# Six pieces of weights instead of three taken apart before the MLPs begin, 2.5 instead of 2 per step, batch 1's attention one step later

## The chip, the cores and the metric

The kernel runs on one core of a Trainium2 chip. The metric is the device time of one execution in microseconds (us). PE is the matmul engine, PEld its weight load, DVE the vector engine, ACT the scalar engine, SP the engine whose queue issues nearly all DMAs. In this chip's profile a granted PE clock of 1.00 stands for the higher of its two levels (2.4 GHz) and 0.50 for the lower (1.2 GHz).

## The reference

```python
# q, k, v: (4 batches, 8 heads, 576, 64); heads 0-3 a local mask (stride 32), heads 4-7 a strided mask
scores = scale * (q @ k.T), masked, softmax
attn_out = softmax @ v                          # (B, H, S, D)
x = attn_out.transpose(0, 2, 1, 3).reshape(2304, 512)
for w_in, w_out in two layers:                  # (512, 2048), (2048, 512)
    h = np.maximum(x @ w_in, 0.0)
    x = (h * h) @ w_out
```

All in float32; the weights and the result are compared at float32 accuracy, so each product is made of three matmuls on rounded high and low parts.

## The kernel before

**The weights' pieces.** The weights arrive as 64-bit words. A layer has 32 pieces of 128 x 512 words, in the order in which they are needed: the `in` piece for column group 0, the `out` piece for row group 0, `in` 1, `out` 1 and so on. Each is taken apart by four operations: `sign_and_end` (two DVE instructions, L213 and L216), `exponent_range` (ACT, L222), `together` (DVE, L227), `in_parts` (ACT L240 makes the high part, DVE L241 the low part). The list `conv` staggers them: in its steady part each run of four operations starts one piece, carries two on and finishes the one that was begun three earlier. `conv_by(n)` issues the next n operations of the list; one whose piece has not been loaded stops it. `ready(key)` issues what is missing if a matmul needs a piece that is not finished in program order.

**The start.** Batch 0's attention (12 fills of packed heads) runs alone, in 15 rounds of eight rows of the table ALONE. After each round the tables START_LOAD and START_CONV say how many pieces are loaded and how many operations of `conv` are issued: 19 in all, which finishes three pieces (0, 1, 2). Batch 0 uses DVE and ACT for its masks, maxima, exponents and divisions, and they are in-order engines, so the pieces' operations stand in the same queues.

**The MLPs.** 72 steps per layer. Step s issues the first product of step s+1 (`mm1`, 12 matmuls, from an `in` piece), then the second product of step s (`mm2`, 12 matmuls, from an `out` piece). Behind `mm1` ACT forms the ReLU and its square (r, sq, gh; L688, L693, L694) and DVE the low part gl (L698). A step has eight points (three inside `mm1`, one behind it, three inside `mm2`, one behind it). At each, `point()` issues the attention of the next batch as far as it is due, and, while the 32 pieces of layer 0 are not done, one operation of `conv`: eight per step, that is two pieces, just what a step uses. The attention of batch 1 is spread by `spans` over points 0 to 116 (steps 0 to 14), that of batches 2 and 3 over the next blocks.

**What sets the order.** Python's order is the order on each engine: there is no scheduler (`manual_schedule`). SP's queue is in order too: `load_ahead(4)` stands at the head of each step, the attention's own loads stand where a fill has freed a buffer.

Of the kernel before, what the change touches and what calls it, by code (L numbers as in the profile page):

```python
# [23 lines left out]
NF = DFF // P  # L24
# [6 lines left out]
NB = len(BLOCKS[0])  # L31
# [10 lines left out]

N_PT = 8

START_LOAD = (0, 0, 0, 1, 0, 1, 0, 1, 0, 1, 1, 1, 1, 2, 2)
START_CONV = (0, 0, 0, 0, 0, 0, 0, 0, 0, 2, 3, 3, 3, 4, 4)
GAP = 80

FIRST_2 = 2
# [93 lines left out]
def tile_attention_then_two_mlps(  # L143
# [34 lines left out]
    half1 = len(pieces) // 2  # L178
# [3 lines left out]
    def load_piece():  # L182

        n = n_load[0]
        if n >= len(pieces):
            return
        kind, layer, f = pieces[n]
        raw[n] = wpool.tile([P, 512, 2], I32, tag=f"w{n % half1}", name="raw")
        n_load[0] += 1
        dst = raw[n].rearrange("p n w -> p (n w)")  # L190
        if kind == "in":
            dst = dst.rearrange("p (c m) -> p c m", c=KC)
            src = w_in[layer].rearrange("(c p) m -> p c m", p=P)[:, :, 2 * f * P:2 * (f + 1) * P]
        else:
            src = w_out[layer][f * P:(f + 1) * P, :]
        nc.sync.dma_start(out=dst, in_=src)

    def load_ahead(n):

        while n and n_load[0] < min(half1, n_part[0] + AHEAD):  # L200
            load_piece()
            n -= 1
# [46 lines left out]
    n_conv, n_part = [0], [0]  # L249

    def conv_by(n):

        while n and n_conv[0] < len(conv):
            fn, i = conv[n_conv[0]]
            if i >= n_load[0]:
                return
            fn(i)
            n_conv[0] += 1
            n -= 1
            n_part[0] += fn is in_parts  # L260
# [25 lines left out]
    def load_qk():  # L286
        i = n_in[0]
        if i >= NFILL:
            return
        n_in[0] += 1  # L290
        qk = src_of(i)[0]
        tag = "qk" + str(i % 3 if i < SPLIT else 0)
        kin[i] = fpool.tile([P, QKW if tag == "qk2" else 4 * KW], F32, tag=tag, name="qk", bufs=1)
        nc.sync.dma_start(out=kin[i][:, :qk.shape[-1]], in_=qk)
# [76 lines left out]
    def load_v():  # L371
        i = n_vin[0]
        if i >= NFILL:
            return
        n_vin[0] += 1
        _, v = src_of(i)
        vin[i] = fpool.tile([P, VW], F32, tag="v", name="v", bufs=5)
        nc.sync.dma_start(out=vin[i][:, :v.shape[-1]], in_=v)
# [240 lines left out]
    def att_to(n):  # L619
        while n_att[0] < n:  # L620
            for fn, i in att[n_att[0]]:
                fn(i)
            n_att[0] += 1
# [31 lines left out]
    def block_x(k):  # L655
        layer, j = blocks[k]
        return (xh[j], xl[j]) if layer == 0 else xin[k]

    def mm1(s, point):

        if s >= len(steps):
            return
        k, f = steps[s]
        ne = tiles_of(k)
        n = TB // ne
        x_hi, x_lo = block_x(k)
        if n_att[0] < len(att):
            ps = ps_h.tile([P, TB], F32, tag="h", name="ps_h")
        else:
            ps = ps_a.tile([P, TB], F32, tag="a", name="ps_h")  # L670
        for c in range(KC):
            for e in range(ne):
                w = ready(("in", blocks[k][0], f + e))
                for i, (a, x) in enumerate(((0, x_hi), (0, x_lo), (1, x_hi))):

                    nc.tensor.matmul(  # L676
                        ps[:, e * n:(e + 1) * n],
                        lhsT=w[:, a, c * P:(c + 1) * P],
                        rhs=x[:, c, :n],
                        start=c == 0 and e == 0 and i == 0,  # L680
                        stop=c == KC - 1 and i == 2 and e == ne - 1,
                    )
                    one_small()
            if c < KC - 1:
                point()
        r = gpool.tile([P, TB], F32, tag="r", name="r", bufs=1)
        sq = gpool.tile([P, TB], F32, tag="sq", name="sq", bufs=1)
        nc.scalar.activation(out=r, in_=ps, func=AF.Relu, scale=W_BACK)  # L688
        h = gpool.tile([P, TB], F32R, tag="gh", name="gh", bufs=2)
        lo = gpool.tile([P, TB], F32R, tag="gl", name="gl", bufs=2)  # L690
        if 0 < n_load[0] - n_part[0]:

            nc.scalar.activation(out=sq, in_=r, func=AF.Square)  # L693
            nc.scalar.activation(out=h, in_=sq, func=AF.Copy)  # L694
        else:
            nc.scalar.activation(out=h, in_=r, func=AF.Square)  # L696
            nc.vector.tensor_tensor(out=sq, in0=r, in1=r, op=ALU.mult)  # L697
        nc.vector.tensor_tensor(out=lo, in0=sq, in1=r32(h), op=ALU.subtract)  # L698
        gh[s], gl[s] = h, lo

    def mm2(s, point):
        k, f = steps[s]
        layer, j = blocks[k]
# [51 lines left out]
                y_at.setdefault(s + 3 * i + 2 * c, []).append((fn, k, c))  # L755


    spans = [(b * NF * N_PT, ((b + 1) * NF - 1) * N_PT - 4) for b in range(3)]

    with tc.manual_schedule():  # L760
        nc.scalar.dma_start(out=cst, in_=consts)
        for n in range(5):
            if n < 3:
                load_qk()
            load_v()
        rounds = 0
        while n_att[0] < att_end[0]:
            att_to(min(n_att[0] + len(ALONE), att_end[0]))
            load_ahead(START_LOAD[rounds])
            conv_by(START_CONV[rounds])  # L770
            rounds += 1
        def nothing():
            pass

        mm1(0, nothing)
        for s in range(len(steps)):
            k, f = steps[s]
            layer, j = blocks[k]
            n_pt = [0]
            load_ahead(4)  # L780
            for fn, k2, c in y_at.get(s, ()):
                fn(k2, c)

            def point(s=s, layer=layer, j=j, f=f):
                n_pt[0] += 1
                at = N_PT * s + n_pt[0]
                for b, (p0, p1) in enumerate(spans):
                    if at > p0:
                        lo, hi = att_end[b], att_end[b + 1]
                        att_to(min(hi, lo + -(-(hi - lo) * (at - p0) // (p1 - p0))))  # L790
                if n_part[0] < half1 or (layer == 1 or j == NB - 1 and f > 2) and n_pt[0] % 4:
                    conv_by(1)

            mm1(s + 1, point)
            point()
            mm2(s, point)
            point()
            if layer == 0 and j == NB - 1:
                for _ in range(2):
                    load_piece()  # L800
# [36 lines left out]
```

## Time and profile before

| what | us |
|---|---|
| median of three runs | 936.99 (934.66 to 937.49) |
| the profiled execution | 935.01 |
| its span (first to last instruction) | 933.1 |
| PE busy | 899.3 (96%) |
| DVE busy | 459.8 (49%) |
| ACT busy | 410.8 (44%) |

The span is one launch on one core. Matmuls are pipelined and their ends are modelled, so the busy time of PE overlaps itself and the idle time in front of an instruction tells more than the share. The start of the program (0 to 40 us) is batch 0's attention; layer 0's steps follow, the first 15 of them (45 to about 175 us) with the taking apart of weights and batch 1's attention beside them.

### The profile page before, as it was taken

The numbers are of one execution on the slowest core, as the hardware profiler recorded it, in microseconds if no ns is written. First come the engines' busy times: TensorE is split into PE (matmuls) and PEld (weight loads), VectorE is DVE, ScalarE is ACT, GpSimd is POOL, SyncE is SP. The second block draws the span as 40 slices with busy tenths as digits, with TensorE's granted clock in tenths as the row PEclk, the third lists the DMA queues.
The fourth block names the chain that finished last, engine by engine and source line by source line (L and its number), as shares of the span: only waits on it lengthen the run. The fifth ranks groups of instructions, "written<-read, shape, count | busy, mean of one in ns | idle before, by whom it ended". The sixth has DMA issues, their size and how long they took to land.

```text
span 933.1 us, 12404 instructions
## 1 busy us (share of the span) xinstructions
PE 899.3 (96%) x4624; PEld 753.7 (81%) x4624; DVE 459.8 (49%) x1196; ACT 410.8 (44%) x863; POOL 0.2 (0%) x4
## 2 busy tenths in 40 slices
PE   8788888899999999999999999999999999999998
PEld 7666667687788888899888888888888888888897
DVE  5867677466675765422268877322222223222221
ACT  6666566355554554332367676332223222322222
POOL 0000000000000000000000000000000000000000
PEclk9799999999999999999999999999999999999999
DMA  8854351022222211010366530001001000100010
GB/s 255 292 168 147 129 182 42 29 84 74 68 91 77 88 46 56 1 47 1 125 213 208 199 113 12 12 27 41 15 9 69 1 22 1 57 6 6 1 46 23
DMA packets 43884, 71.91 MB, mean 77 GB/s; under 512 B 3504, under 2 KB 28208, under 8 KB 43824
## 3 DMA queue, kind: packets, MB, share of 16 engines
q1 hardware_dynamic: 43680, 70.86, 22.9%
q8 instruction: 37, 0.61, 0.3%
q10 hardware_dynamic: 144, 0.26, 0.1%
q14 instruction: 23, 0.19, 0.1%
HBM read 61.67 MB, written 9.44 MB: 76 GB/s over the span
## 4 chain that ended last, share of the span: by engine, by line
PE 88%; DVE 6%; ACT 4%; issue 1%; DMA 1%; SPq 0%; DVEq 0%; ACTq 0%
PE ps_h L676 43%; PE ps_y L731 37%; PE ps_o L477 3%; PE ps_s L418 2%; PE ps_pt L461 1%; ACT r L688 1%; PE ps_s L324 1%; DVE gl L698 1%; ACT sq L693 1%; DVE raw L216 1%; DVE w L241 1%; ACT gh L694 1%; PE ps_x L523 1%; DVE val L227 1%; DVE s L438 1%
## 5 line engine op out<-in xcount | busy, mean ns | idle before, releaser
L676 PE MATMUL ps_h<-xh,w 128*128 128x512 f32 (+1 forms) x1280 | 406.9, 378 | 18.3 <-DVE w L241 13.2
L676 PEld LDWEIGHTS ps_h<-xh,w 128*128 128x128 f32 x1280 | 234.8, 190 | 64.3 <-DVE w L241 18.4
L688 ACT ACTIVATE r<-ps_h 128x512 f32<-128x512 f32 x144 | 86.3, 599 | 406.0 <-PE ps_h L676 383.6
L676 PE MATMUL ps_h<-xl,w 128*128 128x512 f32 (+1 forms) x640 | 238.4, 373 | 0.0
L697 DVE TENSOR_TENSOR sq<-r 128x512 f32<-128x512 f32 x106 | 73.3, 692 | 328.5 <-ACT r L688 328.2
L731 PE MATMUL ps_y<-gh,w 128*128 128x512 f32 (+1 forms) x640 | 155.5, 375 | 0.0
L731 PE MATMUL ps_y<-w,gh 128*128 128x512 f32 x576 | 144.6, 389 | 0.0
L698 DVE TENSOR_TENSOR gl<-sq,gh 128x512 fp32r<-128x512 f32 x144 | 99.7, 692 | 79.3 <-ACT gh L694 65.3
L676 PEld LDWEIGHTS ps_h<-xl,w 128*128 128x128 f32 x640 | 121.9, 191 | 16.9
L731 PEld LDWEIGHTS ps_y<-w,gh 128*128 128x128 f32 x576 | 107.6, 188 | 22.0
L731 PEld LDWEIGHTS ps_y<-gh,w 128*128 128x128 f32 x640 | 108.4, 189 | 16.7
L731 PE MATMUL ps_y<-gl,w 128*128 128x512 f32 (+1 forms) x320 | 84.9, 374 | 0.0
L731 PE MATMUL ps_y<-w,gl 128*128 128x512 f32 x288 | 79.1, 389 | 0.0
L696 ACT ACTIVATE gh<-r 128x512 fp32r<-128x512 f32 x106 | 67.2, 634 | 3.4
L731 PEld LDWEIGHTS ps_y<-w,gl 128*128 128x128 f32 x288 | 54.0, 188 | 11.2
L731 PEld LDWEIGHTS ps_y<-gl,w 128*128 128x128 f32 x320 | 55.2, 189 | 8.9
L454 ACT ACTIVATE s<-s,m 96x128 f32<-96x128 f32 (+2 forms) x176 | 56.0, 387 | 5.1 <-DVE m L438 4.3
L477 PEld LDWEIGHTS ps_o<-v,pt 128*96 128x96 f32 (+2 forms) x352 | 44.7, 181 | 5.4 <-ACT pt L469 0.5
L241 DVE TENSOR_TENSOR w<-val,w 128x512 fp32r<-128x512 f32 x64 | 43.7, 684 | 4.1 <-ACT w L240 4.0
L222 ACT ACTIVATE raw<-raw 128x512 f32<-128x512 f32 x64 | 42.9, 670 | 6.1 <-DVE raw L216 6.1
L216 DVE SCALAR_TENSOR_TENSOR raw<-raw 128x512 int32<-128x512 int32 x64 | 44.4, 694 | 2.2
L477 PE MATMUL ps_o<-v,pt 128*96 128x65 f32 (+2 forms) x352 | 43.8, 258 | 0.1
(36 smaller groups left out, 582.0 us busy)
## 6 DMA issues: line engine op xcount, KB each, us to landing
raw<-moe_w_in_d SPq DMA_DIRECT2D x32, 512.0 KB, 5.1
raw<-moe_w_out_d SPq DMA_DIRECT2D x32, 512.0 KB, 3.8
qk<-loc_qk_d SPq DMA_DIRECT2D x12, 416.0 KB, 3.0
out_d<-o SPq DMA_DIRECT2D x18, 256.0 KB, 2.0
y_dram<-o SPq DMA_DIRECT2D x16, 256.0 KB, 2.0
y_in<-y_dram SPq DMA_DIRECT2D x16, 256.0 KB, 3.4
qk<-loc_qk_d SPq DMA_DIRECT2D x12, 304.0 KB, 3.6
v<-loc_v_d SPq DMA_DIRECT2D x24, 130.0 KB, 3.1
```

The source lines that it names most:

```text
L216: nc.vector.scalar_tensor_tensor(out=lower, in0=upper, scalar=-(2 ** 31), in1=lower, op0=ALU.bitwise_and, op1=ALU.bitwise_or)
L222: nc.scalar.activation(out=upper, in_=upper, func=AF.Copy, scale=2.0 ** (W_EXP // 8 - 112))
L241: nc.vector.tensor_tensor(out=w[:, 1], in0=v, in1=r32(w[:, 0]), op=ALU.subtract)
L418: nc.tensor.matmul(sv[:, h, g], lhsT=t[:, (h * ng + g) * nq:(h * ng + g + 1) * nq], rhs=t[:, 2 * ng * nq + g * ks:2 * ng * nq + g * ks + n ...
L454: nc.scalar.activation(out=blk, in_=blk, func=AF.Exp, scale=-1.0, bias=m[:nq, j:j + 1])
L477: nc.tensor.matmul(ps[:nq, j * W:(j + 1) * W], lhsT=pt[:nk, j * nq:(j + 1) * nq], rhs=t[:nk, j * W:(j + 1) * W], start=True, stop=True,)
L676: nc.tensor.matmul(ps[:, e * n:(e + 1) * n], lhsT=w[:, a, c * P:(c + 1) * P], rhs=x[:, c, :n], start=c == 0 and e == 0 and i == 0, stop=c ...
L688: nc.scalar.activation(out=r, in_=ps, func=AF.Relu, scale=W_BACK)
L696: nc.scalar.activation(out=h, in_=r, func=AF.Square)
L697: nc.vector.tensor_tensor(out=sq, in0=r, in1=r, op=ALU.mult)
L698: nc.vector.tensor_tensor(out=lo, in0=sq, in1=r32(h), op=ALU.subtract)
L731: nc.tensor.matmul(y, lhsT=lhsT, rhs=rhs, start=f == 0 and c not in seen, stop=end and m == last[c])
```

## The change

START_LOAD and START_CONV are other tables: 30 operations instead of 19 are issued before the steps, beginning in round 7 instead of round 9, so that six pieces are done and three more begun. In the steps, while layer 0's pieces last, points 4 and 8 issue two operations and the others one: ten per step, 2.5 pieces. Batch 1's attention is spread over points 8 to 116 instead of 0 to 116.

```diff
-START_LOAD = (0, 0, 0, 1, 0, 1, 0, 1, 0, 1, 1, 1, 1, 2, 2)
-START_CONV = (0, 0, 0, 0, 0, 0, 0, 0, 0, 2, 3, 3, 3, 4, 4)
+START_LOAD = (0, 0, 0, 1, 0, 1, 1, 1, 1, 1, 1, 1, 2, 2, 2)
+START_CONV = (0, 0, 0, 0, 0, 0, 0, 2, 2, 2, 3, 4, 5, 6, 6)
+
+START_ATT = 1
...
-    spans = [(b * NF * N_PT, ((b + 1) * NF - 1) * N_PT - 4) for b in range(3)]
+    spans = [((b * NF or START_ATT) * N_PT, ((b + 1) * NF - 1) * N_PT - 4) for b in range(3)]
...
-                if n_part[0] < half1 or (layer == 1 or j == NB - 1 and f > 2) and n_pt[0] % 4:
+                if n_part[0] < half1:
+                    conv_by(1 if n_pt[0] % 4 else 2)
+                elif (layer == 1 or j == NB - 1 and f > 2) and n_pt[0] % 4:
                     conv_by(1)
```

The first place is DVE at the end of the start: what stands in front of the division (den, xn) of the last of batch 0's twelve fills, whose xn the last transpose in front of `mm1(0)` reads. raw are a piece's words, val its joined words, w its two parts. Lines 213, 216, 227 and 241 of before are lines 215, 218, 229 and 243 of the changed kernel. Before:

```order
L227 SCALAR_TENSOR_TENSOR val_604<-raw_314 128x512
L241 TENSOR_TENSOR w_606<-val_571,w_606 128x512
L213 TENSOR_SCALAR raw_525<-raw_525 128x512
L216 SCALAR_TENSOR_TENSOR raw_525<-raw_525 128x512
L508 TENSOR_SCALAR den_623<-ps_o_616 108x2
L509 RECIPROCAL den_623<-den_623 108x2
L511 TENSOR_TENSOR xn_626<-ps_o_616,den_623 108x128
```

Changed:

```order
L243 TENSOR_TENSOR w_618<-val_540,w_618 128x512
L215 TENSOR_SCALAR raw_489<-raw_489 128x512
L218 SCALAR_TENSOR_TENSOR raw_489<-raw_489 128x512
L229 SCALAR_TENSOR_TENSOR val_624<-raw_400 128x512
L243 TENSOR_TENSOR w_626<-val_588,w_626 128x512
L510 TENSOR_SCALAR den_641<-ps_o_634 108x2
L511 RECIPROCAL den_641<-den_641 108x2
L513 TENSOR_TENSOR xn_644<-ps_o_634,den_641 108x128
```

Three pieces are finished (w) in front of that division instead of one, four values put together instead of two, six pieces begun instead of five.

The second place is DVE from the gl of step 1 to that of step 2 (gl is the low part of what ACT made of `mm1`). Before:

```order
L698 TENSOR_TENSOR gl_717<-sq_714,gh_716 128x512
L213 TENSOR_SCALAR raw_630<-raw_630 128x512
L216 SCALAR_TENSOR_TENSOR raw_630<-raw_630 128x512
L227 SCALAR_TENSOR_TENSOR val_734<-raw_569 128x512
L241 TENSOR_TENSOR w_743<-val_702,w_743 128x512
...
L241 TENSOR_TENSOR w_786<-val_734,w_786 128x512
L698 TENSOR_TENSOR gl_796<-sq_793,gh_795 128x512
```

Changed:

```order
L700 TENSOR_TENSOR gl_731<-sq_728,gh_730 128x512
L243 TENSOR_TENSOR w_735<-val_679,w_735 128x512
L215 TENSOR_SCALAR raw_650<-raw_650 128x512
L218 SCALAR_TENSOR_TENSOR raw_650<-raw_650 128x512
L229 SCALAR_TENSOR_TENSOR val_751<-raw_616 128x512
L243 TENSOR_TENSOR w_756<-val_722,w_756 128x512
...
L243 TENSOR_TENSOR w_791<-val_751,w_791 128x512
L215 TENSOR_SCALAR raw_705<-raw_705 128x512
L218 SCALAR_TENSOR_TENSOR raw_705<-raw_705 128x512
L700 TENSOR_TENSOR gl_806<-sq_803,gh_805 128x512
```

Before, the piece finished first behind gl 1 (w_743) is number 4, which the very next `mm1(2)` reads; now it is number 6 (w_735), which `mm1(3)` reads, one step on, and three pieces instead of two are finished there.

## Rows read from the trace of the kernel before

**Rows 1.** The page: busy time of the engines

```profile
PE 899.3 (96%) x4624; PEld 753.7 (81%) x4624; DVE 459.8 (49%) x1196; ACT 410.8 (44%) x863; POOL 0.2 (0%) x4
```

**Rows 2.** Waits of PE, 45 to 175 us (total us, times, longest)

```profile
PE ps_h L676 <- DVE w L241: 13.2, 12, 1.9
PE ps_h L676 <- ACT w L240: 4.2, 5, 1.5
```

**Rows 3.** Timeline of PE (start, us, what, [idle before]): `mm1` of steps 2, 14, 15

```profile
53.61 0.50 PE L676 MATMUL ps_h<-xh,w 128*128 128x512 f32 x1 [1.55 <-ACT w L240]
...
165.61 0.50 PE L676 MATMUL ps_h<-xh,w 128*128 128x512 f32 x1 [1.91 <-DVE w L241]
...
172.95 0.47 PE L676 MATMUL ps_h<-xh,w 128*128 128x512 f32 x1
```

**Rows 4.** Stretch of 13 steps: PE, PEld, DVE, ACT, POOL busy, PEclk, DMA share, GB/s

```profile
53.61:172.95 119.34, 103.81 (x545) 81.86 (x546) 84.78 (x245) 71.84 (x161) 0.00 (x0) 0.97 0.37 120
```

**Rows 5.** Waits of DVE, 53.61 to 172.95 us

```profile
DVE gl L698 <- ACT gh L694: 27.1, 13, 4.1
```

**Rows 6.** Stretches of 10 us in which the clock fell (columns as rows 4)

```profile
90.00:100.00 10.00, 8.96 (x43) 7.04 (x41) 5.78 (x20) 4.60 (x10) 0.00 (x0) 0.83 0.31 103
...
160.00:170.00 10.00, 8.09 (x35) 6.20 (x34) 5.93 (x13) 4.70 (x10) 0.00 (x0) 0.84 0.05 15
```

**Rows 7.** Timeline of DVE in the start

```profile
22.27 0.26 DVE L438 CUSTOM_DVE_ANT_0 s<-ps_s,cst 108x108 f32<-108x108 f32 x1
...
23.48 0.16 DVE L508 TENSOR_SCALAR den<-ps_o 126x4 f32<-126x4 f32 x1 [0.75 <-PE ps_o L477]
...
26.90 0.41 DVE L213 TENSOR_SCALAR raw<-raw 128x512 int32<-128x512 int32 x1
...
39.46 0.29 DVE L511 TENSOR_TENSOR xn<-ps_o,den 108x128 f32<-108x128 f32 x1
...
46.74 0.69 DVE L698 TENSOR_TENSOR gl<-sq,gh 128x512 fp32r<-128x512 f32 x1 [1.86 <-ACT gh L694]
```

**Rows 8.** Timeline of PE in the start

```profile
39.81 0.44 PE L523 MATMUL ps_x<-cst,xn 108*128 108x108 f32 x1 [1.98 <-DVE xn L511]
39.94 0.78 PE L676 MATMUL ps_h<-xh,w 128*128 128x512 f32 x1
```

**Rows 9.** Timeline of DVE in one step

```profile
87.42 0.69 DVE L698 TENSOR_TENSOR gl<-sq,gh 128x512 fp32r<-128x512 f32 x1 [2.60 <-ACT gh L694]
88.03 0.28 DVE L438 CUSTOM_DVE_ANT_0 s<-ps_s,cst 96x128 f32<-96x128 f32 x1
...
88.87 0.42 DVE L213 TENSOR_SCALAR raw<-raw 128x512 int32<-128x512 int32 x1
89.33 0.69 DVE L216 SCALAR_TENSOR_TENSOR raw<-raw 128x512 int32<-128x512 int32 x1
89.94 0.68 DVE L227 SCALAR_TENSOR_TENSOR val<-raw 128x512 int32<-128x512 int32 x1
90.54 0.68 DVE L241 TENSOR_TENSOR w<-val,w 128x512 fp32r<-128x512 f32 x1
91.14 0.41 DVE L565 TENSOR_TENSOR xl<-ps_x,xh 128x64 fp32r<-128x64 f32 x2
91.47 0.42 DVE L213 TENSOR_SCALAR raw<-raw 128x512 int32<-128x512 int32 x1
...
92.54 0.15 DVE L508 TENSOR_SCALAR den<-ps_o 96x4 f32<-96x4 f32 x1
...
93.27 0.68 DVE L227 SCALAR_TENSOR_TENSOR val<-raw 128x512 int32<-128x512 int32 x1
```

**Rows 10.** Stretches of the start (columns as rows 4)

```profile
15.00:20.00 5.00, 5.00 (x56) 5.00 (x55) 4.59 (x33) 4.50 (x17) 0.00 (x0) 1.00 0.94 301
```

**Rows 11.** DMA of the tiles `raw` (a piece's words), 0 to 60 us

```profile
DMA to landing us min/median/max: 4.5/5.3/7.5
```

## The prediction

> **What bounds the kernel now.** The page comes first: PE is 96% busy and DVE 49% [rows 1], so the kernel is a PE kernel on average, and an edit that only moves DVE and ACT work can win nothing but PE's idle time. PE's waits, between 45 and 175 us, say where that is: 12 waits for the low part of a weight piece (DVE w L241, 13.2 us) and 5 for the high part (ACT w L240, 4.2 us), together 17.4 us [rows 2]. The timeline shows their shape: the first matmuls of a step's `mm1` stand and wait for the `in` piece, 1.55 us in front of `mm1(2)` and up to 1.91 us later, until steps are free of it at 175 us [rows 3]. With three pieces in hand and two made per step, the piece that `mm1(s+2)` reads is finished by the last operations of step s, and they stand on DVE behind gl(s+1): the wait is one of lead, not of throughput. For over these 13 steps (119.34 us, 9.18 us each) DVE is busy only 84.78 us [rows 4], and it stands 27.1 us, 2.1 us per step, at the head of its queue with gl, waiting for ACT's gh [rows 5]. Behind that gl stand the pieces' operations. So DVE idles first and is late afterwards.
>
> The idle PE also costs clock. In the stretches 90 to 100 and 160 to 170 us the granted clock is 0.83 and 0.84 [rows 6], that is some 10 x 0.17 = 1.7 and 1.6 us of full-speed work lost, 3.3 us together, both behind such waits; the other waits did not lower it.
>
> The Trainium skill, "TensorE: Matmul & The Clock Gate", § HAM oscillation — how this bites in real kernels, states that waits between bursts of matmuls re-throttle the array and the next burst starts at half speed. Here the trace agrees in 2 of some 15 steps only; if every wait did it, the part given back would be several times the 3.3 us, which the rows exclude.
>
> **The change part by part.** All is reckoned in the profiled execution's own time, 935.0 us (span 933.1 and 1.9 around it); the median of the runs, 937.0, lies 2.0 above it.
>
> *The start.* 30 operations instead of 19 are issued before the steps. On DVE that is nine pieces begun instead of seven, seven joined instead of four, six finished instead of three. From one step's timeline, start to start: beginning a piece takes 1.07 us (88.87 to 89.94), joining 0.60, finishing 0.60 [rows 9]; a whole piece 2.27 us. The extra is 2 x 1.07 + 3 x 0.60 + 3 x 0.60 = 5.7 us of DVE. In front of the last fill's division stand one begun, two joined and two finished more (the first place in the order): 1.07 + 1.2 + 1.2 = 3.5 us. PE's last transpose waits for just that division (xn at 39.46 us; PE stood 1.98 us for it) and `mm1(0)` follows at 39.94 [rows 7, 8]. From 26.90 us on, when the first piece is begun, DVE paces the start, so I let `mm1(0)` move by the whole 3.5 us. From below: the first two pieces are begun at about 22.3 instead of 26.9 us, and there DVE has a wait of 0.75 us that they fill [rows 7], so 2.7. From above: with DVE late from 22.3 us on, PE stalls 4.6 us sooner, and if its clock falls to half that much sooner too, PE's small matmuls over those 4.6 us take twice as long: 3.5 + 4.6 = 8.1 us. I stay at 3.5, since DVE, not PE, is what the start's last division stood behind.
>
> The other 2.2 us of DVE come between that division and gl(0). In before DVE waited 1.86 us for gh there [rows 7]; that hides most of it, and gl(0) is read only by the last four matmuls of `mm2(0)`, behind a whole `mm1(1)`. I cost it at 0; without that cover it is 0.4 us.
>
> The four more loads in the start run on SP's queue beside the attention's. A piece lands 4.5 to 7.5 us after its issue [rows 11] and is needed two rounds (over 4 us, and longer now that DVE is behind) later at the least; cost 0, see the rivals for what happens if not.
>
> *The steps.* The lead grows from just in time to three pieces and by half a piece with each step: `mm1(3)` reads piece 6, finished right behind gl 1, one step ahead (the second place in the order). The 17.4 us of waits for w go, and with them what the clock lost, 3.3 us. What is late next is DVE itself. A step's DVE work will be 2.5 x 2.27 = 5.7 for pieces, 0.61 for gl, and for one fill 0.84 of maxima, 0.73 of division and 0.33 of xl [rows 9]: 8.2 us. PE's work in such a step is (119.34 - 15.5 idle - 3.3 clock) / 13 = 7.7 us [rows 4, 6], and some 0.2 more as the same attention is spread over 108 points instead of 116: 7.9. So for the steps 1 to 9, until the 98 remaining operations are issued at ten per step, DVE falls 0.3 us per step behind, 2.7 us in all, and its wait for gh is used up. The consumers bear that: a piece has over a step of slack, gl nearly one, and the psum buffers of the attention about four points (3 to 4 us). I take 1.5 us of new PE waits, between 0 (all absorbed) and 4.0 (nothing absorbed and DVE's own waits for ACT of some 0.1 us per step on top). After step 9 DVE has only 2.5 us per step and PE sets the pace. Batch 1's attention beginning at step 1 costs and saves nothing more: the same instructions, the same end (point 116), and step 0 is free for the pieces.
>
> *The sum.* 935.0 + 3.5 - 17.4 - 3.3 + 1.5 = 919.3 us by the profiled execution. The executions of a kernel spread by some 3 us and the profiled one was among the quick ones; I predict 920.
>
> **The rivals.**
> - *DVE takes over as the bound.* If half of its wait for gh stays (1.0 us per step), a step of 1 to 9 takes 8.2 + 1.0 = 9.2 us, as before. Then only the four or five last steps gain: 17.4 / 14 = 1.24 us each, 5.6, and one of the clock's falls, 1.6: 935.0 + 3.5 - 7.2 = 931. For it: DVE and ACT are in order, and gl now has more around it. Against it: DVE waited because it had nothing else to do in front of gl; with ten operations per step it gets there later, and a lead of a step frees PE from it.
> - *Slower.* DVE keeps the whole wait of 2.1 us at gl. Then a step of 1 to 9 is 8.2 + 2.1 = 10.3 us against 9.18, nine times 1.1 = +10; the last steps give 7.2 back, the start takes 3.5: 935.0 + 10 - 7.2 + 3.5 = 941. It decides when DVE's busy time and wait add up instead of filling each other, that is if gh is itself late because PE waits for the pieces again. Against it stands the lead: gh depends on `mm1`, and that on pieces finished a step before.
> - *The loads hold up the start.* Between 15 and 20 us the DMA engines are 0.94 busy at 301 GB/s [rows 10]. Pieces 2, 3 and 4 are now queued about one round sooner, in front of the loads of the last fills; at 0.524 MB each that is 1.74 us per piece, 5.2 us in all. If the fills' own lead does not cover it, the start takes 5.2 instead of 3.5: 921. The Trainium skill, "DMA: Bandwidth & Descriptors", § Queues, rings and completion order, states that each DMA engine takes descriptors in ring order, so a piece queued in front of a fill's load is moved in front of it; it is the reason why I take that delay as possible at all, and nothing in the sum rests on it.
>
> **How the numbers follow.** The forecast (917 to 926 by the bounds of its terms: 935.0 - 20.7 + 2.7, and + 8.1 + 4.0) 0.72, the DMA rival 0.06 (also inside), DVE as the bound 0.14, slower 0.05, the rest, all within 0.3% of before, 0.03. 0.3% is about what a measurement of this kernel can tell from no change (2.8 us). The low end, 914, is 917 less the 3 us by which executions of before differ. The high end, 931, is the DVE rival. Faster 0.91, same 0.04, slower 0.05.
>
> **What would show it.** Right: the waits of PE's L676 (now L678) for w fall from 17.4 us to under 3; `mm1(0)` begins at 42.5 to 45 us; DVE's wait for gh falls from 27 us to under 12 and its busy share rises to over 0.9 between 55 and 130 us; the clock stays at 1.00 in the steps; the first block ends 15 to 18 us sooner, and everything behind it is shifted as a whole. Wrong: a start that is 6 or more us longer with the clock at 0.50 from 25 us on; new waits of PE for DVE's xn, den or xl or for a psum buffer between steps 1 and 9; steps of 9 us there with DVE busy without a gap; waits of DVE's `sign_and_end` for a DMA.

## The result and the profile after

The changed kernel takes 915.59 us (median of four runs, 914.88 to 915.88) against 936.91 us before (four runs, 934.66 to 937.49): a ratio of 0.9776, 95% interval 0.9759 to 0.9793. The profiled execution took 914.88 us, with a span of 913.1 us, 20.0 less than before. The forecast was 920, so the direction and the place were right and the gain was 4 us larger than the sum.

The page's first part of the changed kernel, against [rows 1]:

```profile
PE 890.9 (98%) x4624; PEld 750.8 (82%) x4624; DVE 460.9 (50%) x1200; ACT 409.7 (45%) x859; POOL 0.2 (0%) x4
```

The work is the same on every engine, to about 1 us on DVE and ACT; what went is idle time of PE. PE's waits of the changed kernel from the first ReLU (46.66 us) to the sixteenth (157.08 us), against [rows 2]:

```profile
PE ps_pt L463 <- DVE den L510: 1.6, 1, 1.6
PE ps_o L479 <- ACT pt L471: 1.5, 2, 0.9
PE ps_h L678 <- ACT r L690: 0.7, 1, 0.7
PE ps_pt L463 <- DVE xl L567: 0.2, 1, 0.2
```

No wait for a weight piece is left. The 0.7 us for r stands in both kernels. New are 3.3 us for the attention's tiles (den, the softmax's divisors; pt, its transposed weights; xl, the low part of what it hands to the MLPs). The ReLU of a step (ACT r) is a good milestone, since it starts when a first product ends. Its starts on the two timelines, in us:

| ReLU | before | after | after - before |
|---|---|---|---|
| 0 | 44.79 | 46.66 | +1.87 |
| 3 | 67.42 | 63.55 | -3.87 |
| 6 | 96.71 | 88.40 | -8.31 |
| 10 | 133.10 | 121.77 | -11.33 |
| 15 | 177.04 | 157.08 | -19.96 |
| 19 | 200.35 | 180.37 | -19.98 |

The start loses 1.9 us, the 15 steps give 21.8 back, and from there on everything is shifted by 20.0.

DVE in the stretch that was forecast to be full (columns as in rows 4):

```profile
55.00:120.00 65.00, 61.77 (x356) 50.89 (x355) 63.80 (x186) 52.68 (x114) 0.00 (x0) 1.00 0.57 184
```

DVE is busy 63.80 of 65 us, the granted clock is 1.00. From ReLU 3 to 10 a step takes (121.77 - 63.55) / 7 = 8.3 us, where DVE's work was reckoned at 8.2. DVE's wait for gh, 27.1 us in [rows 5], is this in the changed kernel (46.66 to 157.08 us):

```profile
DVE gl L700 <- ACT gh L696: 2.9, 3, 1.4
```

The start: PE's last transpose and the first matmul of the MLPs, against [rows 8]:

```profile
41.03 0.44 PE L525 MATMUL ps_x<-cst,xn 108*128 108x108 f32 x1 [2.59 <-DVE xn L513]
41.16 0.77 PE L678 MATMUL ps_h<-xh,w 128*128 128x512 f32 x1
```

It is 1.22 us later, not 3.5 (counted from a mark in the start, in the experiments below, it is 1.4). The rest of the 1.87 us is clock. The stretch 44 to 46 us, of before

```profile
44.00:46.00 2.00, 1.31 (x6) 0.76 (x5) 0.85 (x2) 1.18 (x2) 0.00 (x0) 1.00 0.89 323
```

and of the changed kernel

```profile
44.00:46.00 2.00, 2.00 (x7) 1.52 (x5) 2.00 (x5) 1.13 (x2) 0.00 (x0) 0.50 1.02 341
```

Before, the clock was back at 1.00 before `mm1(0)` ended; now all of `mm1(0)` ran at the lower level.

### The profile page after: what moved, and what is told of

It is laid out like the page before. It is cut to its first block, busy times and chain, and to the rows that moved or that the text cites. A ratio compares the mean times of both kernels' runs of the same rounds, so it can differ in the third digit from the quotient of the medians.

```text
span 913.1 us, 12429 instructions
## 1 busy us (share of the span) xinstructions
PE 890.9 (98%) x4624; PEld 750.8 (82%) x4624; DVE 460.9 (50%) x1200; ACT 409.7 (45%) x859; POOL 0.2 (0%) x4
## 4 chain that ended last, share of the span: by engine, by line
PE 88%; DVE 9%; ACT 2%; issue 1%; DMA 0%; ACTq 0%; DVEq 0%
PE ps_h L678 41%; PE ps_y L733 40%; PE ps_o L479 2%; DVE raw L218 2%; PE ps_pt L463 1%; PE ps_s L420 1%; PE ps_s L326 1%; DVE val L229 1%; DVE w L243 1%; DVE gl L700 1%; DVE raw L215 1%; PE ps_x L525 1%; ACT r L690 1%; DVE s L440 1%; ACT sq L695 0%
## 5 line engine op out<-in xcount | busy, mean ns | idle before, releaser
L678 PE MATMUL ps_h<-xh,w 128*128 128x512 f32 (+1 forms) x1280 | 402.5, 375 | 0.7 <-ACT r L690 0.7
L699 DVE TENSOR_TENSOR sq<-r 128x512 f32<-128x512 f32 x110 | 76.2, 693 | 341.7 <-ACT r L690 341.4
L733 PE MATMUL ps_y<-gh,w 128*128 128x512 f32 (+1 forms) x640 | 158.6, 377 | 0.0
L698 ACT ACTIVATE gh<-r 128x512 fp32r<-128x512 f32 x110 | 69.7, 634 | 3.5
L224 ACT ACTIVATE raw<-raw 128x512 f32<-128x512 f32 x64 | 43.2, 675 | 13.0 <-DVE raw L218 12.8
L479 PE MATMUL ps_o<-v,pt 128*96 128x65 f32 (+2 forms) x352 | 42.5, 253 | 1.5 <-ACT pt L471 1.5
```

What stands on the lines that cost most here:

```text
L224: nc.scalar.activation(out=upper, in_=upper, func=AF.Copy, scale=2.0 ** (W_EXP // 8 - 112))
L479: nc.tensor.matmul(ps[:nq, j * W:(j + 1) * W], lhsT=pt[:nk, j * nq:(j + 1) * nq], rhs=t[:nk, j * W:(j + 1) * W], start=True, stop=True,)
L678: nc.tensor.matmul(ps[:, e * n:(e + 1) * n], lhsT=w[:, a, c * P:(c + 1) * P], rhs=x[:, c, :n], start=c == 0 and e == 0 and i == 0, stop=c ...
L733: nc.tensor.matmul(y, lhsT=lhsT, rhs=rhs, start=f == 0 and c not in seen, stop=end and m == last[c])
```

## The experiments

All times are medians beside runs of the kernel before on the same chip; its medians in the three groups were 935.56 (first four), 935.31 (next four) and 934.83 us (last two). Where two kernels of different groups are compared, "by the ratios" is the difference of their ratios to the kernel before, times 935 us. The 95% intervals of the ratios are some 2 to 5 us wide, so a single difference of 1 to 2.5 us between two of the changed kernels is not clear of noise by itself.

**One part alone, and the change without one part.** Start tables alone:

```diff
-START_ATT = 1
+START_ATT = 0
-conv_by(1 if n_pt[0] % 4 else 2)
+conv_by(1)
```

> The new start tables alone: six pieces before the steps, then two per step as before, attention from step 0. Theory (lead): a lead of three pieces that does not grow is enough, since PE only has to be a step behind the pieces; the waits of PE for w (17.4 us before) fall to under 1 us, DVE has 7.1 us of work per step and PE sets the pace: 913 to 917 us. Rival (rate): the waits went because 2.5 pieces are made per step; at two per step DVE again finishes each piece behind gl and most waits stay: 925 us or more.

Measured 911.76 us, ratio 0.9743 (0.9724 to 0.9762): faster than the whole change. From the first ReLU to the sixteenth PE waited only here, beside the 0.7 us for r:

```profile
PE ps_o L479 <- ACT pt L471: 0.6, 1, 0.6
```

So a lead that does not grow is enough, and the faster rate is not needed for it. The rate alone, with the two start tables of before:

```diff
-START_ATT = 1
+START_ATT = 0
```

> The old start tables with 2.5 pieces per step, attention from step 0. Theory (lead): the start is as before (first matmul of the MLPs at 39.9 us); the waits for w stay in the first two to four steps (about 4 us) and vanish when the lead has grown to more than a piece; DVE is full until about step 12: 917 to 921 us. Rival (rate): the faster rate is all that counts and the start's cost is saved: 913 us or less. If DVE's fullness rules instead, the waits are replaced by others and it is 925 or more.

Measured 914.08 us, 0.9769 (0.9750 to 0.9789), between the two theories: better than the 917 to 921 of lead, not quite the 913 or less of rate. The waits for w went at once, but for those in front of `mm1(2)`; where DVE is full, PE waits for its den. Of PE's waits, 45 to 185 us:

```profile
PE ps_pt L463 <- DVE den L510: 1.5, 2, 1.3
PE ps_h L678 <- DVE w L243: 1.2, 1, 1.2
...
PE ps_h L678 <- ACT w L242: 0.4, 1, 0.4
```

So either edit alone removes the stall, the faster rate because 2.5 pieces are made per step and two used, which builds a lead of its own; the two do not add. The change with the attention from step 0 (`START_ATT = 0`, nothing else):

> The changed kernel with batch 1's attention beginning at step 0, as before the change. Theory: DVE is full in the steps 1 to 9, so work put into step 0 (where DVE still waits 1.3 us for gh) fills that wait and the attention is thinner later: within 1.5 us of the changed kernel, either way (914 to 917). Rival: the later start carries a part of the gain because it keeps step 0 free for the pieces: 918 or more.

Measured 913.23 us, 0.9760 (0.9741 to 0.9779), 2.4 us less than the changed kernel (1.5 by the ratios) and just below the expected band. Nothing speaks for a gain by the later attention, and something for a cost (from ReLU 0 to 15 this kernel takes 108.37 us, the changed one 110.42). Nine operations per step instead of ten:

```diff
-conv_by(1 if n_pt[0] % 4 else 2)
+conv_by(1 if n_pt[0] % 8 else 2)
```

> The changed kernel with nine operations per step instead of ten (2.25 pieces). DVE's work in a step falls from 8.2 to 7.6 us, below PE's 7.7 to 7.9, and lasts until step 11. Theory (DVE is the bound of the steps 1 to 9 in the changed kernel): its 3.3 us of PE waits for DVE and ACT go, and steps take 7.7 instead of 8.3 us there: 911 to 914 us. Rival (rate): a lower rate brings waits for w back: 917 or more.

Measured 913.11 us, 0.9763 (0.9739 to 0.9787). That is 2.5 us less than the changed kernel (1.2 by the ratios), and with two pieces and the same attention it is 912.83 (below); with the attention from step 0, ten operations took 913.23 and eight 911.76. None of these differences is clear by itself, but each has the same sign: once the lead is there, a faster rate gains nothing and seems to cost 1 to 2.5 us, with DVE full and PE waiting for it. The theory's sizes were missed: PE's listed waits are 2.9 us against 4.0 (the 3.3 us for the attention's tiles fell to 2.2 and did not go), and a step from ReLU 3 to 10 takes (118.49 - 62.71) / 7 = 8.0 us, not 7.7.

**How much lead, and what it costs in the start.** The kernels of this part make two pieces per step and begin the attention at step 0. Four pieces instead of six before the steps:

```diff
-START_CONV = (0, 0, 0, 0, 0, 0, 0, 2, 2, 2, 3, 4, 5, 6, 6)
+START_CONV = (0, 0, 0, 0, 0, 0, 0, 1, 2, 2, 3, 3, 4, 4, 4)
```

> The new loads, but 23 operations before the steps (four pieces instead of six), two pieces per step, attention from step 0. Theory (lead): one piece of lead is enough, since a piece is finished in the middle of the step before it is read; no waits for w, and the start is 1 us or more shorter than with six pieces (DVE has 3.6 us less to do there): 910 to 912 us. Rival: the lead of one piece is eaten when DVE falls behind in the steps with all of attention, and some waits for w come back: 914 to 918.

Measured 909.74 us, 0.9728 (0.9716 to 0.9741): the best of all, 5.9 us less than the changed kernel (4.5 by the two ratios). One piece of lead is enough. The start is 1.2 us shorter than with six pieces, as expected (40.26 - 22.48 = 17.8 us from the mark that is explained below, against 19.0). PE's waits between 45 and 185 us are this row and no other; the second is a stretch of its steps:

```profile
PE ps_h L678 <- ACT r L690: 0.7, 1, 0.7
```

```profile
52.00:130.00 78.00, 77.88 (x451) 65.28 (x451) 70.41 (x211) 60.22 (x139) 0.00 (x0) 1.00 0.54 175
```

Two operations more than before the change, that is half a piece of lead:

```diff
+START_CONV = (0, 0, 0, 0, 0, 0, 0, 1, 2, 2, 3, 3, 3, 3, 4)
```

> 21 operations before the steps, only two more than before the change; two pieces per step, attention from step 0. The piece that the next first product reads is then finished two operations sooner, right behind gl instead of four DVE instructions behind it (1.7 us sooner). Theory (a wait is as long as the piece is late, 1.24 us on average): nearly all waits for w go with 1.7 us of lead, at most 3 us in total stay: 909 to 912 us. Rival (the piece must stand in front of gl, whose wait for gh is what delays it): half of the waits or more stay, 918 or more.

Measured 915.03 us, 0.9789 (0.9772 to 0.9805). PE's listed waits for w (one of them put down to a DMA) fell from 17.4 to 3.2 us, as the theory wanted, yet the time is 3 us above its band. The waits of the weight loads (PEld), 45.30 to 157.88 us, tell why:

```profile
PEld ps_h L678 <- DVE w L243: 6.5, 8, 1.4
PEld ps_h L678 <- ACT r L690: 1.1, 1, 1.1
PEld ps_h L678 <- ACT w L242: 1.0, 3, 0.4
```

There are 11 waits for w, not four; the seven that are not listed in front of the matmuls last 0.24 to 0.53 us here, too short to show between matmuls whose ends are modelled. The control, as many operations as before in the start but begun in round 7 and with the new loads:

```diff
+START_CONV = (0, 0, 0, 0, 0, 0, 0, 1, 2, 2, 2, 3, 3, 3, 3)
```

> A control: as many operations before the steps as before the change (19, three pieces), but begun from round 7 on and with the new, earlier loads; two pieces per step, attention from step 0, so each step's order is that of the kernel before. Theory (lead): the waits for w stay at 15 us or more and the time is 933 to 937 us, at most 2 us less than before through the start. Rival (the earlier loads or the early rounds carry the gain): 925 or less.

Measured 935.12 us, 1.0004 (0.9993 to 1.0015): nothing. Its waits are those of the kernel before, to the tenth of a microsecond:

```profile
PE ps_h L678 <- DVE w L243: 13.2, 12, 1.9
PE ps_h L678 <- ACT w L242: 4.2, 5, 1.5
```

Neither the earlier loads nor the earlier rounds matter by themselves; the lead does. Six pieces, but none of the 30 operations in rounds 7 and 8:

```diff
+START_CONV = (0, 0, 0, 0, 0, 0, 0, 0, 0, 3, 5, 5, 5, 6, 6)
```

> The new start tables with the same 30 operations, but none in rounds 7 and 8 (from round 9 on, as before the change), two pieces per step, attention from step 0. Theory (the start cost less than forecast because DVE's waits of rounds 7 and 8 were filled): the first matmul of the MLPs comes about 1 us later after the first fill's mask than with operations from round 7, and the time is 912 to 914. Rival (DVE's sum of work alone counts): no difference, 911.8 within 0.5.

Measured 913.54 us, 0.9769 (0.9756 to 0.9781), 1.8 us above the same kernel with operations from round 7. Taken from one mark (the last of PE's transposes of a local fill's xn, at 23.61 here, 23.35 there, 22.05 in the changed kernel, 22.23 before) the last transpose follows 22.3 us later, against 19.0, 19.0 and 17.6 (17.1 and 17.0 in the two experiments with the start tables of before). So in the profiled executions the early rounds save 3.3 us of start, more than the 1 us expected. By the medians it is the 1.8 us (2.4 by the ratios): the profiled execution, 915.51 us, was the slowest of the five. The operations are also denser from round 9 on, and what that alone costs was not tried. In its start PE stands behind ACT as well:

```profile
35.34 1.97 PE L479 MATMUL ps_o<-v,pt 126*126 126x65 f32 x8 [1.64 <-ACT pt L471]
...
45.94 0.44 PE L525 MATMUL ps_x<-cst,xn 108*128 108x108 f32 x1 [2.58 <-DVE xn L513]
```

**The later attention.** With the start tables and two pieces per step (`START_ATT = 1`):

> The new start tables, two pieces per step, but batch 1's attention from step 1. Theory (the late attention costs only where DVE is full, because the denser attention then makes DVE fall behind its psum buffers): with 7.1 us of DVE per step there is room, and it is within 1 us of the same kernel with attention from step 0 (911.8): 911 to 913. Rival (the late attention costs by itself, PE having less to fill step 0 and more later): 2 us or more above, 913.5 to 915.

Measured 912.83 us, 0.9765 (0.9752 to 0.9778), 1.1 us above the same kernel with attention from step 0. And alone, in the kernel before:

```diff
-    spans = [(b * NF * N_PT, ((b + 1) * NF - 1) * N_PT - 4) for b in range(3)]
+    spans = [((b * NF or 1) * N_PT, ((b + 1) * NF - 1) * N_PT - 4) for b in range(3)]
```

> The kernel before with only the attention's later start (batch 1's from step 1). Theory (lead): the lead is unchanged, so PE's waits for w stay at 15 us or more, somewhat larger where the denser attention delays DVE: 935 to 939 us. Rival (the empty step 0 gives the pieces a lead): waits fall by a third or more, 932 or less. Also a count of the price of a wait: if each listed wait costs 0.3 us beyond its idle time, the time from the first to the sixteenth ReLU (132.25 us before), less the listed waits and what the clock lost, stays at 111 to 112 us; if not, it falls to 106 to 107.

Measured 937.76 us, 1.0026 (1.0011 to 1.0041): a little slower. PE's three largest waits, 45 to 185 us:

```profile
PE ps_h L676 <- DVE w L241: 10.3, 12, 1.8
PE ps_h L676 <- ACT w L240: 2.5, 4, 1.5
PE ps_o L477 <- ACT pt L469: 1.4, 2, 0.8
```

The waits for w came to 12.8 us, less than the 15 or more expected. The trace does not show a cost of the later attention in the first steps. In the profiled execution (933.88 us, one of the quickest) ReLU 15 comes at 172.01 us, 5.0 sooner than before, since the waits are shorter and the clock did not fall; 3.9 us of that are lost again in the second layer, at four waits that no other kernel's trace lists (185 to 925 us; o is ACT's copy of a result, which stands there for an earlier store):

```profile
PE ps_y L731 <- ACT o L740: 2.1, 4, 0.7
```

And the two executions with a mean clock of 0.994 took 932.87 and 933.88 us, the ten with 0.986 to 0.991 took 936.36 to 940.30. So the 2.4 us of these medians cannot be put down to the later attention, and this run does not price it.

The two other pairs do, from ReLU 0 to 15: with two pieces 108.03 us against 106.69, with 2.5 pieces 110.42 against 108.37, that is 1.3 and 2.0 us, of which PE's listed waits are 1.1 and 1.7. That it costs with two pieces too, where DVE is busy 89.2 of 108.0 us, speaks against the theory that it costs only where DVE is full; but 912.83 us lies in that theory's band, so this is not settled. The four kernels with the later attention show two waits of PE for pt (1.4 to 1.5 us), those with attention from step 0 one of 0.6 to 0.7 or none. That the denser placing over the points causes them was not tried.

## Why the prediction was right, and where its sum was off

- *The wait is one of lead, not of throughput*: right. Without lead the waits stay (the control, 935.12 us); with one piece they are gone (909.74 us). The faster rate, which builds a lead, removes them as well (914.08 us). That the lead grows with each step, to which the prediction gave weight, was not needed (911.76 us with a lead that does not grow).
- *17.4 us of waits go*: the step whose size was wrong. The waits went, but they cost more than the idle time listed in front of the matmuls. Take the time from ReLU 0 to 15, less PE's listed waits, less what the clock lost there (3.3 us before by rows 6; 5.1 in the control, by its granted clock in stretches of 10 us, 0.83, 0.83, 0.90 and 0.93; none in the others):

| kernel | ReLU 0 to 15 | listed waits of PE (count) | rest |
|---|---|---|---|
| before | 132.25 | 18.1 (18) | 110.9 |
| control, 19 operations | 133.87 | 18.1 (18) | 110.7 |
| later attention alone | 127.27 | 15.4 (21) | 111.9 |
| half a piece of lead | 112.58 | 3.9 (5) | 108.7 |
| the change | 110.42 | 4.0 (5) | 106.4 |
| six pieces, two per step | 106.69 | 1.3 (2) | 105.4 |
| four pieces, two per step | 106.20 | 0.7 (1) | 105.5 |

The same matmuls should leave the same rest. It is 5 to 6.5 us larger where there are some 20 waits: about 0.3 us for each. (With half a piece of lead it is 3 us larger by waits that are not listed, see above.) The price was stated for the later attention alone before it ran (111 to 112, measured 111.9). Where the 0.3 us stand, a single wait, the one at 165.61 us of the kernel before, shows ([rows 3] has its row). The matmuls around it:

```profile
163.07 0.40 PE L676 MATMUL ps_h<-xh,w 128*128 128x512 f32 x1
163.30 0.40 PE L676 MATMUL ps_h<-xl,w 128*128 128x512 f32 x1
```

and the weight loads:

```profile
163.07 0.19 PEld L676 LDWEIGHTS ps_h<-xl,w 128*128 128x128 f32 x1
165.61 0.19 PEld L676 LDWEIGHTS ps_h<-xh,w 128*128 128x128 f32 x1 [2.35 <-DVE w L241]
```

Matmuls follow each other by 0.23 us (163.07 to 163.30), but each is drawn 0.40 long, so the next was due at 163.53, not 163.70: 2.08 us lost where 1.91 is listed. And the first one behind a wait is drawn 0.50 instead of 0.40: another 0.1. Together 0.27, by this one wait. PE's weight loads, whose ends are not drawn over their successors, list more, before (44.79 to 177.04 us):

```profile
PEld ps_h L676 <- DVE w L241: 18.4, 14, 2.4
PEld ps_h L676 <- ACT w L240: 7.0, 8, 2.0
```

25.4 us there against 17.4 in [rows 2]; the price by this estimate, 17.4 + 17 x 0.27 = 22.0, lies between. The Trainium skill, "Perfetto Trace Analysis", § Identifying the Most-Contended Engine, says that matmul busy time is a bad measure of how close a kernel is to its limit, because matmuls are pipelined, and names the busy share of LDWEIGHTS (and the share of the peak rate) instead. This trace agrees: for the same 4624 matmuls PE is busy 899.3 us before and 890.9 after, its weight loads 753.7 and 750.8. The idle time in front of the matmuls misleads too, as shown.

- *The clock gives 3.3 us back*: right. It is 1.00 from 50 us on in the changed kernel.
- *The start costs 3.5 us*: too much; 1.2 to the first matmul, 1.9 to the first ReLU (from the mark 1.4 against the kernel before, up to 2.0 against the other executions with its tables). The extra DVE work in front of the last division was nearly right (3.0 us busy), but DVE had more room than the one wait of 0.75 us. DVE from the mask at 22.27 us to that division, before

```profile
22.27:39.46 17.19, 12.47 (x87) 11.09 (x87) 14.98 (x65) 12.38 (x40) 0.00 (x0) 0.73 0.91 290
```

and from the same place in the changed kernel:

```profile
22.08:40.69 18.61, 11.24 (x87) 10.04 (x87) 17.99 (x72) 14.53 (x44) 0.00 (x0) 0.80 0.95 324
```

DVE does 3.0 us more in a stretch that is only 1.4 longer: 2.2 us of gaps became 0.6. Without the early rounds the price was 3.3 us higher in the profiled executions. The bound with the clock did not come: PE stalled from 24 us on, as feared, but the clock stayed at 1.00 until about 33 us.
- *1.5 us of new waits*: too little; 3.3 us listed, about 4.4 with 0.27 for each of the four, over the 4.0 that was the upper bound. The mechanism was the one named: DVE full in the steps 1 to 9 at 8.3 us per step (8.2 forecast), so that its wait for gh disappears and PE waits for den, xl and, behind ACT, pt.
- *The later attention costs and saves nothing*: it saves nothing and seems to cost 1 to 2 us, see above.
- The sum with what was measured: 935.0 + 1.9 - (22.0 + 3.3) + 4.4 = 916.0, against 914.9; 1.1 us are not accounted for. By the bounds of its own terms the forecast ended at 917: the sum gave the 17.4 us of waits no bounds, and only the 3 us that were added for the spread of the executions took 915.6 into the range.
- The rivals. DVE as the bound came true in place and not in price, 8.3 us per step instead of 9.2, since DVE waited for no gh between 53 and 123 us. The slower case stayed away for the same reason. The loads held nothing up in the changed kernel: PE waited for none of the fills' loads behind the first.
- The signs. `mm1(0)` began at 41.16 us and not at 42.5 to 45, and the first block ended 20.0 us sooner and not 15 to 18. Of the signs of being wrong one came, PE's waits for den and xl, but with 1.8 us too small to matter.

## What to carry to other kernels

When an engine stalls once per step for a product of another engine that is itself half idle, ask first for lead, not for rate: here four operations (one piece) moved ahead of the loop gave 25.6 us. A faster rate alone gave 21.5, more pieces ahead 23.8, both edits 21.3: none did better than the one piece. Work put ahead of a loop is cheapest in the rounds where its engine still has gaps, so begin it there. Price a stall of PE by the next start that was due: here the idle time behind a modelled end listed too little (17.4 us), the gaps of its weight loads too much (25.4), for some 22.

## What the runs showed of the hardware that was not expected

A wait of PE for a weight piece cost about 0.3 us beyond the idle time listed in front of the matmul (0.27 worked out at one wait; rest of 110.7 to 111.9 us with 18 to 21 waits, 105.4 to 105.5 with one or two). The granted clock stayed at 1.00 through PE stalls of 1.03, 0.89 and 0.72 us in the start (25 to 31 us) and fell in one of 1.70 us there (32 to 34 us); in the kernel with the later attention alone 21 waits of up to 1.8 us cost no clock at all in the profiled execution (1.00 from ReLU 0 to 15), while runs of that kernel spread from 932.9 to 940.3 us and their mean clock from 0.994 down to 0.986.
